# Chunked attention into a gated FFN: turned tiles written in a row, earlier clears, other load order, last store in two pieces

## The chip, the cores and the metric

The kernel runs on one core of one Trainium2 chip. The core has TensorE (PE, matrix products into PSUM), VectorE (DVE), ScalarE (ACT), GpSimd (POOL) and SyncE (SP, which here only issues transfers). The metric is the device time of one execution in microseconds, as the median of several runs.

## The reference

Queries attend by chunks of 32 tokens. A chunk sees 8 memory slots and the keys from 16 tokens before its start to 8 behind its end. The result, with the heads side by side, goes through an FFN with a ReLU gate.

```
q, k, v: (4, 8, 768, 64)      mem_k, mem_v: (4, 8, 8, 64)
for c in range(768 // 32):
    l, r = max(0, 32*c - 16), min(768, 32*c + 32 + 8)
    scores = q[:, :, 32*c:32*c+32] @ concat(mem_k, k[:, :, l:r]).T / 8
    a = softmax(scores)
    out[:, :, 32*c:32*c+32] = a @ concat(mem_v, v[:, :, l:r])
x = out as (3072, 512)
y = (relu(x @ w_gate) * (x @ w_val)) @ w_out        # d_ff = 1536
```

## The kernel before

The 3072 tokens are cut into eight blocks of 384 (half a sequence each), numbered 0 to 7. A block has 4 groups of 96 queries (`NQ`, `QB`), each against 128 key rows: 8 memory slots and a band of 120 tokens. Heads are taken in four pairs (`hp`). All matrix products are in f16 with f32 sums.

For every head pair the kernel needs keys and queries with the head dimension on partitions ("turned"). Blocks 0, 1 and 2 turn them on PE: `turn_pe` (L177) multiplies rows, held as 4 tokens per partition (`J` = 4), by a selection matrix `sel` (L191, keys) or by the identity `ident` (L196, queries). The product of step j is written to PSUM at every fourth column, so that the columns come out in token order. `turn_copy` (L199) has DVE cast them to f16: one copy of 896 elements for blocks 0 and 2 (L207), two for block 1 (L209, L210). Blocks 3 to 7 are turned by DMA (`turn_dma`).

The scores go to PSUM (`step_s0` for block 0, `step_s` for the others, both by `score_mms` L236), ACT takes the exponential. In blocks 0 and 1 `wide_d` (L279, L281) makes the sums and their logarithm, `wide_e` (L285) their inverse, `wide_v` (L292, L294) the weighted values, and DVE their product, `xT`. From block 2 on the value tile `vwins` carries ones in the upper half of its columns, so that values and sums come out of one product (`step_v`, L301). `one_words` (L447) writes these ones over the first two blocks' value tiles; for block 2 that is the code at L551 to L553, behind the last FFN unit of block 0.

The FFN of a block is 12 units of 128 hidden columns (L337; ACT's ReLU at L343, DVE's product at L344) and three output units of 128 tokens (`out_unit`, L362 to L367: 12 products, a copy by ACT, a store from ACT's queue).

The order is written out by hand: every engine runs its instructions in program order, and the framework adds the waits. Block 0's attention runs ahead of everything (L457 to L504, with products on a `filler` tile to occupy PE while loads are on their way). Then the FFN of block n is interleaved with the attention of block n+1 (L521 to L550 for the first, `run`, L580, for the rest). In `run` a turn of block 2 stands one unit ahead of its scores, and shares their PSUM tile `sc`.

Loads go through three queues. SP and ACT load the f32 rows of heads 0 to 3 for block 0 (`kst`, `qst`, L383, L384). POOL issues all others, casting to f16 on the way: first `memv`, then the rows of heads 4 to 7 (`load_rows`, L127, L128), then, behind the building of `ident` and `sel` (L433, L434), the values (`load_band`, L136), `memk` and the FFN's weights in six column slices (`load_w`, L166). A POOL load waits until the one eight before it has landed. SP copies the memory values into the value tiles (`load_mem_v`, L152).

Of the kernel before, what the change touches and what calls it, by code (L numbers as in the profile page):

```python
# [17 lines left out]
def kernel(  # L18
# [28 lines left out]
    J = 4  # L47
# [66 lines left out]
    def rows_of(n):  # L114
        if n not in rows:
            rows[n] = (half.tile([KR + 2, H, J * D], F16, tag="rk", name="rk"),
                       half.tile([QR, H, J * D], F16, tag="q16", name="rq"))
        return rows[n]

    def load_rows_mem(dma, dst, n, h0, nh):  # L120
        src = bass.AP(tensor=mem_k.tensor, offset=mem_k[n // 2, h0, 0, 0].offset,
                      ap=[[J * D, 2], [NMEM * D, nh], [1, J * D]])
        dma(dst, src)

    def load_rows(n, h0, nh):
        rk, rq = rows_of(n)
        pool_dma(rk[0:KR, h0:h0 + nh], k_rows(n, h0, nh))  # L127
        pool_dma(rq[:, h0:h0 + nh], q_rows(n, h0, nh))  # L128

    def load_band(n, src_t, dsts):  # L130
        b, p = divmod(n, 2)
        for i in range(NQ):
            m0, m1 = (16 if (p == 0 and i == 0) else 0), (112 if (p == 1 and i == NQ - 1) else BAND)
            src = bass.AP(tensor=src_t.tensor, offset=src_t[b, 0, TB * p + QB * i - 16 + m0, 0].offset,
                          ap=[[D, m1 - m0], [S * D, H], [1, D]])
            pool_dma(dsts[p][NMEM + m0:NMEM + m1, i, :, 0:D], src)  # L136

    def fetch_mem(dst, src_t):
        pool_dma(dst, bass.AP(tensor=src_t.tensor, offset=src_t[0, 0, 0, 0].offset,
                              ap=[[D, NMEM], [NMEM * D, B * H], [1, D]]))  # L140
# [33 lines left out]
    def bank(name):  # L174
        return pools["f"].tile([128, 512], F32, tag="f", name=name)

    def turn_pe(n, hp):  # L177

        if n != 1:
            pool, tag = (pools["t"], "t") if n == 0 else (sps, "sc")  # L180
            ps = pool.tile([128, 2, 512], F32, tag=tag, name="kq_ps")
            kps, qps = ps[:, 0], ps[:, 1, 0:TB]
        else:
            ps, kps, qps = None, bank("k_ps"), bank("q_ps")[:, 0:TB]
        turns[n, hp] = ps, kps, qps
        rk, rq = (t.rearrange("p h (j d) -> p h j d", j=J) for t in rows_of(n))
        sel = sels[n % 2].rearrange("p i t -> p (i t)")
        for j in range(J):
            kj = kps.rearrange("p (r j) -> p j r", j=J)[:, j]
            for hh in range(2):  # L190
                nc.tensor.matmul(kj[D * hh:D * hh + D], lhsT=rk[:, 2 * hp + hh, j], rhs=sel[0:KR + 2],  # L191
                                 start=True, stop=True)
        for j in range(J):
            qj = qps.rearrange("p (r j) -> p j r", j=J)[:, j]
            for hh in range(2):
                nc.tensor.matmul(qj[D * hh:D * hh + D], lhsT=rq[:, 2 * hp + hh, j], rhs=ident[:QR, :QR],  # L196
                                 start=True, stop=True)

    def turn_copy(n, hp):  # L199
        if n not in kTs:  # L200
            kq = turned.tile([128, HP, 512 + TB], F16, tag="kq", name="kq")
            kTs[n] = kq[:, :, 0:512].rearrange("p a (i m) -> p i a m", i=NQ)
            qTs[n] = kq[:, :, 512:].rearrange("p a (i m) -> p i a m", i=NQ)
            turns[n] = kq
        ps, kps, qps = turns.pop((n, hp))
        if n != 1:
            dve_copy(turns[n][:, hp], ps.rearrange("p a c -> p (a c)")[:, 0:512 + TB])  # L207
        else:
            dve_copy(turns[n][:, hp, 0:512], kps)  # L209
            dve_copy(turns[n][:, hp, 512:], qps)  # L210

    def turn_dma(n):
        kTs[n] = turned.tile([128, NQ, HP, 128], F16, tag="kT", name="kT")
# [25 lines left out]
    def step_s0(n, hp):  # L239

        sc = sps.tile([128, 2, 512], F32, tag="sc", name="sc_ps")
        mq = bass.AP(tensor=maskq.tensor, offset=maskq.offset, ap=[maskq.ap[0], [0, NQ], [1, QB]])
        for hh in range(2):
            nc.tensor.matmul(sc[:, hh, 0:TB].rearrange("p (i m) -> p i m", m=QB), lhsT=maskk, rhs=mq,
                             start=True, stop=False)
        score_mms(n, hp, sc, False)
        ex = epool.tile([128, 2, NQ, QB], F16, tag="ex", name="ex")
        nc.scalar.activation(ex.rearrange("p h i m -> p h (i m)"), sc[:, :, 0:TB], ACT.Exp, scale=SCALE)
        exs[n, hp] = ex
# [25 lines left out]
    def wide_d(n, hp):  # L275
        ex = exs[n, hp]
        for i0, i1, kind in ((0, 1, 1), (1, NQ, 0)) if n == 0 else ((0, NQ - 1, 0), (NQ - 1, NQ, 2)):
            for hh in range(2):
                nc.tensor.matmul(xs[D * hh:D * hh + D, QB * i0:QB * i1], lhsT=ones[:, kind, :],  # L279
                                 rhs=ex[:, hh, i0:i1, :], start=True, stop=True)  # L280
        nc.scalar.activation(xs, xs, ACT.Ln, scale=1.0 / 64.0)  # L281

    def wide_e(n, hp):
        rinv = rpool.tile([128, TB], F32, tag="rw", bufs=4, name="rw")
        nc.scalar.activation(rinv, xs, ACT.Exp, scale=-1.0, bias=mln64)  # L285
        rinvs[n, hp] = rinv
# [68 lines left out]

    def out_unit(n, t, between=()):
        o_ps = bank("o_ps")
        for m in range(NDC):
            if m == NDC // 2:
                for piece in between:  # L360
                    piece()
            nc.tensor.matmul(o_ps, lhsT=gvs[n][:, m, 128 * t:128 * t + 128], rhs=wo[:, m, :],  # L362
                             start=(m == 0), stop=(m == NDC - 1))
        o_sb = opool.tile([128, DM], F32, name="o_sb")
        nc.scalar.copy(o_sb, o_ps)  # L365
        row0 = TB * n + 128 * t
        act_dma(out[row0:row0 + 128, :], o_sb)  # L367

    def unit(n, u, between=()):
        if u < NDC:  # L370
# [7 lines left out]
            nc.tensor.matmul(xo, lhsT=filler[:, 0:128], rhs=filler[:, 0:TB], start=True, stop=True)  # L378


    nc.scalar.preload_act_table_set("natural_log_exp_and_others")
    for hp in range(HP // 2):
        sp(kst[0:KR, 2 * hp:2 * hp + 2], k_rows(0, 2 * hp, 2))  # L383
        act_dma(qst[:, 2 * hp:2 * hp + 2], q_rows(0, 2 * hp, 2))  # L384
        if hp == 0:
            load_rows_mem(sp, kst[KR:KR + 2], 0, 0, H // 2)
    fetch_mem(memv, mem_v)
    load_rows(0, 4, 4)
    load_rows_mem(pool_dma, rows_of(0)[0][KR:KR + 2, H // 2:H], 0, H // 2, H // 2)

    def words(t):
        return t.bitcast(U32)

    zero(words(ident), 0)
    zero(words(sels[0].rearrange("p i t -> p (i t)")), 0)
    zero(words(filler), 0)


# [21 lines left out]
    def select(ap, fill_with, base, pattern, mult, op=ALU.not_equal):  # L420
        nc.gpsimd.affine_select(out=ap, in_=ap, compare_op=op, fill=fill_with, base=base, pattern=pattern,
                                channel_multiplier=mult)

    def build_sel(p):

        s = sels[p]
        first_row = -6 if p == 0 else 10
        parts = [(0, NQ, 2, 32)] if p == 0 else [(0, NQ, 2, 30), (0, NQ - 1, 30, 32)]
        for i0, i1, t0, t1 in parts:
            select(s[:, i0:i1, t0:t1], 1.0, -first_row - t0, [[-24, i1 - i0], [-1, t1 - t0]], 1)  # L430
        select(s[:, :, 0:2], 1.0, -KR, [[0, NQ], [-1, 2]], 1)

    select(ident, 1.0, 0, [[-1, 128]], 1)  # L433
    build_sel(0)  # L434
    load_band(0, v, vwins)
    load_mem_v(0)
    fetch_mem(memk, mem_k)
# [19 lines left out]
    with tc.tile_pool(name="tps", bufs=2, space=bass.MemoryType.PSUM) as pools["t"]:  # L457
        fill(12)
        cast(0, 0, dve_copy)
        for t, hp in ((1, 0), (1, 1), (0, 1)):  # L460
            cast(t, hp, act_copy)
        turn_pe(0, 0)
        turn_copy(0, 0)
        fill(4)
        step_s0(0, 0)
        turn_pe(0, 1)
        turn_copy(0, 1)
        wide_d(0, 0)
        wide_e(0, 0)
        turn_pe(0, 2)  # L470
        step_s0(0, 1)
        turn_copy(0, 2)
        turn_pe(0, 3)
        turn_copy(0, 3)
    pools["f"] = ctx.enter_context(tc.tile_pool(name="fps", bufs=4, space=bass.MemoryType.PSUM))
    wide_d(0, 1)
    step_s0(0, 2)
    wide_e(0, 1)
    fill(1)
    step_s0(0, 3)  # L480
    wide_v(0, 0)
    wide_d(0, 2)
    wide_e(0, 2)


# [10 lines left out]

    ffn_open(0, (0, 1))
    wide_v(0, 1)
    chunk(0, 0)
    wide_d(0, 3)  # L500
    wide_e(0, 3)
    wide_v(0, 2)
    chunk(0, 1)
    wide_v(0, 3)  # L504
# [12 lines left out]
    def sums(n, hp):  # L517
        wide_d(n, hp)
        wide_e(n, hp)
# [23 lines left out]
    ffn_unit(0, 8)  # L543
    wide_v(1, 1)
    sums(1, 3)
    ffn_unit(0, 9)
    wide_v(1, 2)
    ffn_unit(0, 10)
    wide_v(1, 3)
    ffn_unit(0, 11)  # L550
    one_words(0, 0, 128, 0, NQ, ONE)  # L551
    one_words(0, 0, NMEM + 16, 0, 1, 0)
    one_words(0, 0, NMEM, 0, 1, ONE)  # L553
    load_band(2, v, vwins)
    load_mem_v(2)
    wo_src = moe_w_out.rearrange("(c p) f -> p c f", p=128)
# [87 lines left out]
```

## Time and profile before

| | |
|---|---|
| median of 5 runs | 241.1 us (240.81 to 242.24) |
| the profiled execution's own time | 242.24 us |
| its span | 239.3 us |
| PE busy | 230.1 us, 96% of the span |
| ACT busy | 142.8 us, 60% |
| DVE busy | 105.0 us, 44% |
| POOL busy | 100.2 us, 42% |
| granted PE clock, mean | 0.997 of full |
| DMA | 27.61 MB in 107655 packets |

The span is the stretch that the profiler saw; the execution's own time has some 3 us around it. Lines are those of the kernel before. In a group, "x64 | 4.3, 286" is the count, the busy time in us and the mean of one in ns. What follows the next bar is the idle time in front of the group and what ended it. In a timeline a line starts with its start and its duration in us.

### The profile page before, as it was taken

How to read it: one execution, taken by the hardware profiler on the slowest of the kernel's cores; microseconds unless marked ns; L12 is line 12 of the kernel's file. 1: busy time of each engine (PE TensorE's matmuls, PEld its weight loads, DVE VectorE, ACT ScalarE, POOL GpSimd, SP SyncE). 2: the span in 40 equal slices, each digit the busy share in tenths (PEclk: the TensorE clock that was granted, in tenths of full speed). 3: DMA queues.
4: the chain of work that ended last, by engine and by line, in shares of the span. 5: the costliest groups of instructions: out<-in, count | busy, mean ns of one | idle time of the engine just before them, and what ended most of it. 6: DMA issues, size and time to landing. Idle time of an engine off the chain costs nothing.

```text
span 239.3 us, 4598 instructions
## 1 busy us (share of the span) xinstructions
PE 230.1 (96%) x1737; PEld 133.6 (56%) x1737; DVE 105.0 (44%) x203; ACT 142.8 (60%) x300; POOL 100.2 (42%) x125
## 2 busy tenths in 40 slices
PE   7879999899999999999999999999999999999993
PEld 3635555455644566646664566556664666456641
DVE  4535646878621045512662146504652166313400
ACT  3564595277753388817984589728892698434321
POOL 7997667937039802990089302990040000000000
PEclk9999999999999999999999999999999999999998
DMA  7999999999979999799909997699902100120012
GB/s 160 152 177 195 186 186 189 178 192 146 141 119 116 200 152 143 47 166 124 184 13 126 151 178 68 45 191 148 139 3 78 53 3 0 44 90 0 1 44 88
DMA packets 107655, 27.61 MB, mean 115 GB/s; under 512 B 91682, under 2 KB 104562, under 8 KB 107634
## 3 DMA queue, kind: packets, MB, share of 16 engines
q0 software_dynamic: 82528, 15.16, 79.0%
q1 hardware_dynamic: 21234, 5.48, 20.5%
q10 hardware_dynamic: 3872, 6.69, 8.5%
q8 instruction: 13, 0.21, 0.3%
q14 instruction: 8, 0.07, 0.1%
HBM read 31.13 MB, written 6.29 MB: 156 GB/s over the span
## 4 chain that ended last, share of the span: by engine, by line
PE 83%; DVE 6%; POOL 3%; DMA 3%; ACT 2%; issue 1%; POOLq 0%; DVEq 0%
PE o_ps L362 26%; PE g_ps L337 24%; PE v_ps L337 24%; DMA wv<-in_moe_w_val_dram 3%; PE sc_ps L261 3%; PE xs_ps L301 2%; PE xo_ps L301 2%; DVE kq L207 2%; DVE gv L344 2%; POOL vwin L136 2%; DVE vwin L447 1%; PE sc_ps L236 1%; DVE kq L209 1%; ACT ln L305 1%; PE xo_ps L292 1%
## 5 line engine op out<-in xcount | busy, mean ns | idle before, releaser
L344 DVE TENSOR_TENSOR gv<-v_ps,gr 128x384 f16<-128x384 f32 x95 | 52.8, 557 | 99.6 <-ACT gr L343 85.9
L337 PE MATMUL v_ps<-xT,wv 128*128 128x384 f16 x380 | 78.3, 326 | 0.4 <-DMA wv<-in_moe_w_val_dram 0.2
L337 PE MATMUL g_ps<-xT,wg 128*128 128x384 f16 x380 | 78.4, 326 | 0.0
L362 PE MATMUL o_ps<-wo,gv 128*128 128x512 f16 x288 | 63.5, 379 | 0.0
L343 ACT ACTIVATE gr<-g_ps 128x384 f16<-128x384 f32 x95 | 46.2, 487 | 19.4 <-PE g_ps L337 10.3
L337 PEld LDWEIGHTS <-wv 128*128 128x128 f16 x384 | 36.1, 98 | 22.9 <-DMA wv<-in_moe_w_val_dram 1.4
L337 PEld LDWEIGHTS <-wg 128*128 128x128 f16 x384 | 36.0, 98 | 22.6
L362 PEld LDWEIGHTS <-gv 128*128 128x128 f16 x288 | 28.0, 98 | 33.0
L224 POOL COPY qbd<-qT 64x1536 f16<-64x1536 f16 x10 | 14.6, 1462 | 61.3 <-DMA qT<-q16n 61.0
L365 ACT COPY o_sb<-o_ps 128x512 f32<-128x512 f32 x24 | 14.1, 586 | 41.2 <-PE o_ps L362 37.2
L267 ACT ACTIVATE ex<-sc_ps,bias 128x256 f16<-128x256 f32 x84 | 33.4, 468 | 7.7 <-PE sc_ps L236 7.1
L136 POOL DMA_DIRECT2D vwin<-in_v_dram x32 | 29.0, 932 | 2.9 <-PE g_ps L337 1.0
L310 ACT ACTIVATE rinv<-ln,mln 64x768 f32<-64x768 f32 x24 | 22.2, 923 | 0.0
L305 ACT ACTIVATE ln<-xo_ps 64x384 f32<-64x384 f32 x24 | 11.7, 487 | 14.7 <-PE xs_ps L301 14.7
L136 POOL DMA_DIRECT2D k<-in_k_dram x20 | 17.8, 902 | 0.4 <-issue 0.4
L162 POOL DMA_DIRECT2D q16n<-in_q_dram x20 | 15.6, 800 | 5.0 <-DMA wo<-in_moe_w_out_dram 5.0
L316 DVE TENSOR_TENSOR xT<-xo_ps,rinv 64x384 f16<-64x384 f32 x24 | 13.1, 546 | 10.2 <-ACT rinv L310 10.2
L316 DVE TENSOR_TENSOR xT<-xs_ps,rinv 64x384 f16<-64x384 f32 x24 | 13.2, 551 | 0.7
L301 PEld LDWEIGHTS <-vwin 128*128 128x128 f16 x192 | 10.8, 98 | 3.2
L305 ACT ACTIVATE ln<-xs_ps 64x384 f32<-64x384 f32 x24 | 11.4, 474 | 0.0
L301 PE MATMUL xo_ps<-ex,vwin 128*128 128x96 f16 x96 | 11.1, 206 | 0.0
L301 PE MATMUL xs_ps<-ex,vwin 128*128 128x96 f16 x96 | 11.1, 206 | 0.0
(70 smaller groups left out, 136.3 us busy)
## 6 DMA issues: line engine op xcount, KB each, us to landing
out_dram<-o_sb ACTq DMA_DIRECT2D x24, 256.0 KB
vwin<-in_v_dram POOLq DMA_DIRECT2D x24, 120.0 KB, 8.9
q16n<-in_q_dram POOLq DMA_DIRECT2D x20, 96.0 KB, 5.2
k<-in_k_dram POOLq DMA_DIRECT2D x15, 120.0 KB, 5.0
wg<-in_moe_w_gate_dram POOLq DMA_DIRECT2D x6, 256.0 KB, 8.1
wv<-in_moe_w_val_dram POOLq DMA_DIRECT2D x6, 256.0 KB, 8.4
wo<-in_moe_w_out_dram POOLq DMA_DIRECT2D x3, 512.0 KB, 9.9
rk<-in_k_dram POOLq DMA_DIRECT2D x5, 224.0 KB, 7.7
```

What stands on the lines that cost most here:

```text
L136: pool_dma(dsts[p][NMEM + m0:NMEM + m1, i, :, 0:D], src)
L162: pool_dma(q16s[n][:, i], src)
L224: nc.gpsimd.tensor_copy(qbds[n % 2][s, :, :, hh, :].rearrange("p i a m -> p (i a) m"), qTs[n][s].rearrange("p i a m -> p (i a) m"))
L267: nc.scalar.activation(flat[:, :, :, s], view[:, :, :, s], ACT.Exp, scale=SCALE, bias=bias[:, g:g + 1])
L301: nc.tensor.matmul((xo, xs)[hh][:, QB * i:QB * i + QB], lhsT=vw[:, i, 2 * hp + hh, :], rhs=ex[:, hh, i, :], start=True, stop=True)
L305: nc.scalar.activation(ln[:, hh], (xo, xs)[hh][D:128], ACT.Ln, scale=1.0 / 64.0)
L310: nc.scalar.activation(rinv, lns.pop((n, hp)), ACT.Exp, scale=-1.0, bias=mln64[0:D, :])
L316: nc.vector.tensor_tensor(out=x_of(n)[D * hh:D * hh + D, hp, :], in0=(xo, xs)[hh][0:D], in1=rinv[:, hh, :], op=ALU.mult)
L337: nc.tensor.matmul(ps[a], lhsT=(wg, wv)[a][:, f, 128 * m:128 * m + 128], rhs=xTs[n][:, f, :], start=(f == 0), stop=(f == NFC - 1))
L343: nc.scalar.activation(gr, g_ps, ACT.Relu)
L344: nc.vector.tensor_tensor(out=gvs[n][:, m, :], in0=v_ps, in1=gr, op=ALU.mult)
L362: nc.tensor.matmul(o_ps, lhsT=gvs[n][:, m, 128 * t:128 * t + 128], rhs=wo[:, m, :], start=(m == 0), stop=(m == NDC - 1))
```

## The change

It has five parts.

1. In blocks 1 and 2 a turn's product j is written to PSUM in a row (columns 128 j or 96 j onward). The copy reads PSUM in permuted order, one element from each of the four rows in turn, and writes token order. Block 2 now takes two copies per turn, as block 1 did. Block 0 keeps the stepped write and its one copy.
2. The ones for block 2's value tile are written in pieces between the units 8 to 11 of block 0 in place of all behind unit 11.
3. ACT's table load stands behind its two query loads. POOL clears `ident` and `sel` itself, which DVE did, and builds them ahead of its loads. The rows of heads 4 to 7 are loaded by pairs of heads.
4. In block 0's attention the scores of pair 1 stand ahead of turn 2, the sums of pair 1 ahead of turn 3, the values of pair 0 ahead of the scores of pair 3, the sums of pair 3 ahead of the first FFN chunk; one filler product is gone.
5. The last store is made in two halves: DVE copies the left half, which SP stores, ACT copies and stores the right.

```diff
@@ turn_pe
-        for j in range(J):
-            kj = kps.rearrange("p (r j) -> p j r", j=J)[:, j]
-            for hh in range(2):
-                nc.tensor.matmul(kj[D * hh:D * hh + D], lhsT=rk[:, 2 * hp + hh, j], rhs=sel[0:KR + 2],
-                                 start=True, stop=True)
-        for j in range(J):
-            qj = qps.rearrange("p (r j) -> p j r", j=J)[:, j]
-            ...
+        for t, dst, w in ((rk, kps, sel[0:KR + 2]), (rq, qps, ident[:QR, :QR])):
+            steps = dst.rearrange("p (r j) -> p j r", j=J) if n == 0 else dst.rearrange("p (j r) -> p j r", j=J)
+            for j in range(J):
+                for hh in range(2):
+                    nc.tensor.matmul(steps[D * hh:D * hh + D, j], lhsT=t[:, 2 * hp + hh, j], rhs=w,
+                                     start=True, stop=True)
@@ turn_copy
-        if n != 1:
+        if n == 0:
             dve_copy(turns[n][:, hp], ps.rearrange("p a c -> p (a c)")[:, 0:512 + TB])
         else:
-            dve_copy(turns[n][:, hp, 0:512], kps)
-            dve_copy(turns[n][:, hp, 512:], qps)
+            for src, dst in ((kps, turns[n][:, hp, 0:512]), (qps, turns[n][:, hp, 512:])):
+                dve_copy(dst.rearrange("p (r j) -> p r j", j=J), src.rearrange("p (j r) -> p r j", j=J))
@@ out_unit
-        nc.scalar.copy(o_sb, o_ps)
-        act_dma(out[row0:row0 + 128, :], o_sb)
+        if last:
+            for s, copy, dma in ((slice(0, 256), dve_copy, sp), (slice(256, 512), act_copy, act_dma)):
+                copy(o_sb[:, s], o_ps[:, s])
+                dma(out[row0:row0 + 128, s], o_sb[:, s])
+        else:
+            nc.scalar.copy(o_sb, o_ps)
+            act_dma(out[row0:row0 + 128, :], o_sb)
@@ start
-    nc.scalar.preload_act_table_set("natural_log_exp_and_others")
     for hp in range(HP // 2):
         ...
-    fetch_mem(memv, mem_v)
-    load_rows(0, 4, 4)
-    load_rows_mem(pool_dma, rows_of(0)[0][KR:KR + 2, H // 2:H], 0, H // 2, H // 2)
+    nc.scalar.preload_act_table_set("natural_log_exp_and_others")
-    zero(words(ident), 0)
-    zero(words(sels[0].rearrange("p i t -> p (i t)")), 0)
     ...
+    nc.gpsimd.memset(words(ident), 0)
+    nc.gpsimd.memset(words(sels[0].rearrange("p i t -> p (i t)")), 0)
     select(ident, 1.0, 0, [[-1, 128]], 1)
     build_sel(0)
+    fetch_mem(memv, mem_v)
+    load_rows(0, 4, 2)
+    load_rows_mem(pool_dma, rows_of(0)[0][KR:KR + 2, H // 2:H], 0, H // 2, H // 2)
+    load_rows(0, 6, 2)
     load_band(0, v, vwins)
@@ block 0
+        step_s0(0, 1)
         turn_pe(0, 2)
-        step_s0(0, 1)
         turn_copy(0, 2)
+        wide_d(0, 1)
+        wide_e(0, 1)
         turn_pe(0, 3)
         turn_copy(0, 3)
     ...
-    wide_d(0, 1)
     step_s0(0, 2)
-    wide_e(0, 1)
-    fill(1)
-    step_s0(0, 3)
     wide_v(0, 0)
     wide_d(0, 2)
+    step_s0(0, 3)
     wide_e(0, 2)
     ...
     wide_v(0, 1)
-    chunk(0, 0)
     wide_d(0, 3)
     wide_e(0, 3)
+    chunk(0, 0)
@@ between the units of block 0
     sums(1, 3)
+    one_words(0, 0, 128, 0, 1, ONE)
     ffn_unit(0, 9)
     wide_v(1, 2)
+    one_words(0, 0, NMEM + 16, 0, 1, 0)
+    one_words(0, 0, NMEM, 0, 1, ONE)
     ffn_unit(0, 10)
     wide_v(1, 3)
+    one_words(0, 0, 128, 1, 2, ONE)
     ffn_unit(0, 11)
-    one_words(0, 0, 128, 0, NQ, ONE)
-    one_words(0, 0, NMEM + 16, 0, 1, 0)
-    one_words(0, 0, NMEM, 0, 1, ONE)
+    one_words(0, 0, 128, 2, NQ, ONE)
```

More of the change, by code (lines that the diff above doesn't have):

```diff
@@ L187, in turn_pe @@
         sel = sels[n % 2].rearrange("p i t -> p (i t)")
-        for j in range(J):
-            kj = kps.rearrange("p (r j) -> p j r", j=J)[:, j]
-            for hh in range(2):
-                nc.tensor.matmul(kj[D * hh:D * hh + D], lhsT=rk[:, 2 * hp + hh, j], rhs=sel[0:KR + 2],
-                                 start=True, stop=True)
-        for j in range(J):
-            qj = qps.rearrange("p (r j) -> p j r", j=J)[:, j]
-            for hh in range(2):
-                nc.tensor.matmul(qj[D * hh:D * hh + D], lhsT=rq[:, 2 * hp + hh, j], rhs=ident[:QR, :QR],
-                                 start=True, stop=True)
+        for t, dst, w in ((rk, kps, sel[0:KR + 2]), (rq, qps, ident[:QR, :QR])):
[4 more added lines that the diff above has]
+                                     start=True, stop=True)
     def turn_copy(n, hp):
@@ L357, in out_unit @@
         o_ps = bank("o_ps")
+        last = n == NB - 1 and t == NT - 1
         for m in range(NDC):
```

## The prediction

> **What bounds the kernel now.** I read the page first (engine shares, DMA row), then the chain that ended last from the start, then the groups with shapes kept apart, then the timeline around each place where TensorE (PE) stands still.
>
> ```profile
> span 239.3 us, 4598 instructions
> PE 230.1 (96%) x1737; PEld 133.6 (56%) x1737; DVE 105.0 (44%) x203; ACT 142.8 (60%) x300; POOL 100.2 (42%) x125
> ...
> DMA  7999999999979999799909997699902100120012
> ```
>
> PE is the engine that sets the end: from 82 us to 235.5 us its chain has no gap, so an edit counts only if it moves the moment at which that dense stretch begins, or the tail behind it. The DMA row (one digit is 6 us) says that the 16 DMA engines are 90% busy or more from 6 us to 66 us. In that stretch PE can't run ahead of its weights:
>
> ```profile
> 10.28 6.71 DMA wv<-in_moe_w_val_dram
> 16.99 0.05 issue
> 17.04 0.34 PE v_ps L337
> ```
>
> The first block's FFN starts when its first value weights land, at 16.99. The same happens twice more, and in the first of the two VectorE (DVE) is late at the same moment, since its copies of block 1 run back to back from 23.97 to 27.28:
>
> ```profile
> 26.73 0.55 DVE L210 CAST kq<-q_ps 128x384 f16<-128x384 f32 x1
> ...
> 27.32 0.44 PEld L337 LDWEIGHTS <-wv 128*128 128x128 f16 x4 [0.54 <-DMA wv<-in_moe_w_val_dram]
> 27.33 0.82 PE L337 MATMUL v_ps<-xT,wv 128*128 128x384 f16 x4 [0.16 <-DVE kq L210]
> ...
> 35.88 0.44 PEld L337 LDWEIGHTS <-wv 128*128 128x128 f16 x4 [0.40 <-DMA wv<-in_moe_w_val_dram]
> ```
>
> So up to 36 us the weights are the clock, and time that PE saves before is spent waiting. The next place is the largest stall that is left, 46.85 to 48.22, where DVE works off memsets ahead of the copy that block 2's first scores need:
>
> ```profile
> 42.79 1.67 DVE L447 MEMSET vwin<- 128x1024 uint32 x3 [0.16 <-issue]
> ...
> 44.46 0.27 DVE L559 MEMSET k<- 32x256 uint32 x1
> ...
> 44.82 0.27 DVE L560 MEMSET k<- 32x256 uint32 x1
> ...
> 45.85 0.91 DVE L447 MEMSET vwin<- 128x1024 uint32 x1 [0.16 <-issue]
> ...
> 47.09 1.08 DVE L207 CAST kq<-kq_ps 128x896 f16<-128x896 f32 x1
> ...
> 48.22 0.34 PE L236 MATMUL sc_ps<-kq 64*128 64x96 f16 x8 [1.37 <-DVE kq L207]
> ```
>
> **Part 1, the turns.** The groups give one matmul with 64 weight columns and 96 moving columns, written with a step of four elements (L196) and in a row (L292), and the copies:
>
> ```profile
> L196 PE MATMUL kq_ps<-ident,rq 96*64 96x96 f16 x64 | 4.3, 286 | 0.0
> ...
> L292 PE MATMUL xo_ps<-ex,vwin 128*64 128x96 f16 x64 | 2.9, 210 | 0.6 <-DVE xT L294 0.6
> ...
> L209 DVE CAST kq<-k_ps 128x512 f16<-128x512 f32 x4 | 2.7, 686 | 0.0
> ...
> L210 DVE CAST kq<-q_ps 128x384 f16<-128x384 f32 x4 | 2.2, 547 | 0.0
> ```
>
> In the timeline eight L196 take 0.33 us from first start to the next group (23.72 to 24.05), eight L292 take 0.19 us (34.59 to 34.78): the step costs 0.14. Eight L191 of 128 columns take 0.42 (23.30 to 23.72); in a row, by 128/96 of 0.19, 0.25: 0.17 less. So a turn falls from 0.75 to 0.44 us on PE, 2.5 us over eight turns. Almost none of it reaches the end. In block 1 the scores wait for DVE, whose chain starts with a product (L344, 23.48) that the turns don't move; the last turn's 0.31 is lost before 35.88, where the weights land. In block 2 each copy stands behind a product that waits for ScalarE's queue (L343 behind two L305), so it starts when it did.
>
> The permuted copy isn't in the trace: every DVE read of PSUM there is in a row. A copy takes 547 ns for 384 elements and 686 for 512, so 1.09 ns an element and about 0.13 fixed. The nearest row is PE's stepped write: eight L196 start 41 ns apart though each lasts 286, since the two halves of the partitions run side by side, so each has 82 ns for its 96 elements: 0.86 ns an element with a step, still faster than the copy goes. [...] A gain is excluded: no DVE row with a source in PSUM goes faster than this, in a row as they all are.
>
> For block 2 the one copy of 896 becomes two. From its start to the score the one takes 1.14 us (52.84 to 53.98), the pair in block 1 takes 1.21 (23.97 to 25.18): +0.07 for each of four turns.
>
> **Part 2, the ones' memsets.** One fill of 1024 elements, and the two small ones behind it, stood in one piece ahead of unit (1,0)'s product; half of the fill and both small ones now lie between the units 9 to 11, where DVE has gaps of 0.47 (38.24), 0.64 (39.73) and 0.68 us (41.39), and each memset is 0.27. What stays is a fill of 512: 0.49 by the two rows (0.27 for 256, 0.91 for 1024). The queue from 42.79 is 1.67 - 0.49 = 1.18 us shorter; PE is free by 46.4, so all of it counts: the copy starts at 45.91, the score at 47.12 in place of 48.22, 1.10 less. With +0.07 for the other three turns block 2 gives -0.89. If the gaps were filled, each memset would put off a product by 0.27, which the four PSUM banks let PE run past.
>
> **Part 3, the start.** GpSimd (POOL) now clears and builds the identity and selection before its loads. No POOL memset of that size is in the trace; its 128x1 ones take 0.10, a select over 128x128 0.29; I take 0.15 each. With the selects (0.29 + 0.65) the first load (memv) goes out at about 2.35 in place of 1.42. The rows of heads 4 to 7 were two loads (0.74, 0.68) and are four; with 0.57 for the smallest load as the floor, four of 0.60: +1.0. The selects no longer stand ahead of the v loads (-0.95). So the v loads (5.17) and all behind them, memk and the weights, are issued about 1.0 to 1.1 us later (wg at 10.6, not 9.49). Each POOL load waits for the one eight before it; two more in front shift the partners, but from memk on they are the same ones, and the new waits (third v load on memv, fourth on the first rows) are over by then.
>
> What that does to the landing: POOL's first packets flowed only at 4.6, when the k and q loads of SP and ACT let them, and wg's flowed at 12.0, behind the v packets. A load alone flows about 1.7 us after its issue begins (97.42 to about 99.2). At 10.6 wg's would be there at 12.2: 0.2 later, the rest being queue. Bounds: 0 if the queue still covers it, +1.1 if none of it does. I take +0.2.
>
> The order of block 0 (the score of head pair 1 ahead of turn 2, sums earlier) brings heads' sums forward, so behind the first value weights come 3.35 us to the end of chunk 3 where there are 3.56 now (17.04 to 20.6): with the landing at 17.2, 20.6 as before. The values of pair 0 are now asked for at 13.3 (now 15.09); v landed at about 13 and may make PE wait up to 0.5, hidden by the weights. The +0.2 comes back at 27.3 and 35.9, where later weights land; I count it once. The table load (1.28 us at 0.81) ran beside the query loads' issue (0.84 already); behind them it ends at 3.0, before ScalarE's first cast at 4.90: 0. Filler and first turn start 0.2 earlier, hidden by the weights too.
>
> **Part 4, the last store.** Today: copy 235.49, 0.59 us, issue at 236.10, packets from 236.9 to 237.75. In the changed program ScalarE's half copy waits for DVE's (a wait on DVE is in its list): DVE half at 256 x 1.09 + 0.13 = 0.41, to 235.9; ScalarE's half 0.39 (487 ns for 384 at L343, 586 for 512 at L365), to 236.34; second issue 236.36, 0.26 later than now, but half the packets (-0.42). -0.1, ends -0.4 and +0.3.
>
> **Sum.** +0.2 - 0.89 - 0.1 = -0.8 us, on a profiled execution of 242.24 us (span 239.3 and 2.9 around it): 241.4, span 238.5. That execution was the slowest of five; against the median of 241.1 it is 240.3. A change under 0.5% (1.2 us) counts as none here.
>
> **Rivals.**
> [...]
> 2. The loads aren't covered: POOL's later start leaves DMA engines idle near 4 to 12 us, weights land up to 1.1 later, and values of pair 0 wait besides: 1.1 in place of 0.2, so +0.1 in all: 241.2; with POOL memsets of 0.4 each (+0.5) and a wait for v that isn't hidden (+0.5), 242.2 and above. For it: 363 GB/s from 3 to 4 us, so the first loads finish early. Against: the queue in front of wg.
> 3. PE's turns do pay: without POOL's packets the k and q loads of block 0 are done sooner, weights land no later, DVE's products aren't in front of the copies. Half of the turns' 2.5 us and no +0.2: -0.8 - 0.2 - 1.2 = -2.2, 238.9. Against: DVE is busy without a gap in front of 27.28.
> 4. Nothing arrives: the memsets only move the wait to ScalarE. Within rival 2's time.
>
> **Chances.** The sum holds 0.48 (its own range 239.0 to 241.6, 0.20 of it below 239.9); rival 3 0.20, faster; rival 1 0.19, slower; rivals 2 and 4 0.13, of which 0.06 slower. Faster 0.20 + 0.20 = 0.40, same 0.28 + 0.07 = 0.35, slower 0.19 + 0.06 = 0.25. For 8 in 10 the range takes rival 3 whole, rival 2, and rival 1 up to f = 1.6: 238.4 to 244.0.
>
> **What would show it.** Right: turn matmuls near 206 ns at 96 columns; permuted copies at 686 and 547 ns; the score behind block 2's first turn about 1.1 us earlier against the unit before; the first wv landing between 17.0 and 17.4. Wrong: permuted copies over 900 and 700 ns; a wait of PE for v at about 13.5 longer than 1 us; wv landing past 18; the last packets later than 2.3 us behind the last matmul.

## The result and the profile after

| | before | changed |
|---|---|---|
| median, runs of both side by side | 241.47 us (80 runs, 240.14 to 244.55) | 240.65 us (43 runs, 239.45 to 242.42) |
| profiled execution, its own time | 242.24 us | 239.98 us |
| span of it | 239.3 us | 238.1 us |

The ratio changed to before is 0.9969, with a 95% interval of 0.9957 to 0.9982: 0.31% faster, 0.75 us (the medians are 0.82 apart), and by the bound of 0.5% no change. The forecast was 240.3 us.

The page after, with the engine shares and the DMA row:

```profile
span 238.1 us, 4610 instructions
PE 227.4 (96%) x1736; PEld 131.4 (55%) x1736; DVE 105.5 (44%) x208; ACT 142.3 (60%) x300; POOL 101.6 (43%) x129
...
DMA  7999999999979999499939999499902100120012
```

PE has 2.7 us less to do (230.1 before), and the span is only 1.2 us shorter: part of what PE no longer does, it now waits. The groups of the changed kernel with shapes kept apart show the turns written in a row and the permuted copies (the mean of one, in ns, stands behind the comma):

```profile
L207 DVE CAST kq<-k_ps 128x512 f16<-128x512 f32 x4 | 2.7, 680 | 0.0
...
L193 PE MATMUL q_ps<-ident,rq 96*64 96x96 f16 x32 | 1.4, 206 | 0.0
L207 DVE CAST kq<-q_ps 128x384 f16<-128x384 f32 x4 | 2.2, 546 | 0.0
```

A matmul of 96 columns takes 206 ns (286 stepped), the permuted copies take 680 and 546 ns (686 and 547 in a row). So the permuted read costs nothing.

The chain that ended last has the first value weights in the same place, 0.47 us later than before (16.99):

```profile
10.97 6.50 DMA wv<-in_moe_w_val_dram
17.46 0.05 issue
17.51 0.34 PE v_ps L334
```

PE's timeline around the weights and at the first score of block 2 and the next one:

```profile
13.75 0.23 PE L289 MATMUL xo_ps<-ex,vwin 128*64 128x96 f16 x2 [0.34 <-DMA vwin<-memv]
...
16.51 0.36 PE L276 MATMUL xs_ps<-ex,ones 128*64 128x96 f16 x4 [1.08 <-ACT rw L282]
...
27.25 0.82 PE L334 MATMUL v_ps<-xT,wv 128*128 128x384 f16 x4 [0.18 <-DMA wv<-in_moe_w_val_dram]
...
35.89 0.82 PE L334 MATMUL v_ps<-xT,wv 128*128 128x384 f16 x4 [0.25 <-DMA wv<-in_moe_w_val_dram]
...
46.99 0.34 PE L233 MATMUL sc_ps<-kq 64*128 64x96 f16 x8 [0.50 <-DVE kq L207]
...
52.81 0.34 PE L233 MATMUL sc_ps<-kq 64*128 64x96 f16 x8 [0.51 <-DVE kq L207]
```

The two later waits for value weights end where they ended before (27.33, 35.88). The first score of block 2 is 1.23 us earlier than before (48.22) and the fourth 1.04 (64.46, before 65.50); with 0.16 at the last store, below, that is the whole gain of the profiled executions. Two things are new: at 16.51 PE stands still for 1.08 us for ScalarE, and each of the four scores of block 2 waits 0.50 us for its copy. Before, only the first of the four waited (1.37 us, behind the memsets); the trace puts down no wait to the other three.

DVE's queue ahead of the first of these copies:

```profile
42.69 0.48 DVE L451 MEMSET vwin<- 128x512 uint32 x1
43.16 0.27 DVE L564 MEMSET k<- 32x256 uint32 x1
...
44.55 0.91 DVE L451 MEMSET vwin<- 128x1024 uint32 x1 [0.16 <-issue]
...
45.79 1.14 DVE L207 CAST kq<-kq_ps 128x512 f16<-128x512 f32 x2
```

The fill of 1.67 us has become one of 0.48, and the copy (two of them) starts at 45.79, 1.30 earlier than before (47.09).

The last store in the timeline:

```profile
234.45 0.42 DVE L366 COPY o_sb<-o_ps 128x256 f32<-128x256 f32 x1 [7.14 <-DMA out_dram<-o_sb]
234.90 0.38 SPq L367 DMA_DIRECT2D out_dram<-o_sb  x1
234.91 0.37 ACT L366 COPY o_sb<-o_ps 128x256 f32<-128x256 f32 x1 [2.46 <-DVE o_sb L366]
```

ScalarE's half waits for VectorE's half. From the start of the first copy to the end of the span it is 3.65 us (238.1 - 234.45), before it was 3.81 (239.3 - 235.49).

### The profile page after: what moved, and what is told of

Same layout as the page of the kernel before. It is cut to its first block, busy times and chain, and to the rows that moved or that the text cites. A ratio compares the mean times of both kernels' runs of the same rounds, so it can differ in the third digit from the quotient of the medians.

```text
span 238.1 us, 4610 instructions
## 1 busy us (share of the span) xinstructions
PE 227.4 (96%) x1736; PEld 131.4 (55%) x1736; DVE 105.5 (44%) x208; ACT 142.3 (60%) x300; POOL 101.6 (43%) x129
## 4 chain that ended last, share of the span: by engine, by line
PE 79%; DMA 7%; POOL 5%; DVE 4%; issue 2%; ACT 2%; POOLq 0%; DVEq 0%
PE o_ps L360 25%; PE g_ps L334 23%; PE v_ps L334 23%; DMA wv<-in_moe_w_val_dram 6%; PE sc_ps L258 3%; DVE kq L207 2%; POOL vwin L136 2%; PE xo_ps L298 2%; PE xs_ps L298 2%; DVE gv L341 2%; DMA out_dram<-o_sb 1%; ACT ln L302 1%; ACT gr L340 1%; PE xo_ps L289 1%; POOL rk L127 1%
## 5 line engine op out<-in xcount | busy, mean ns | idle before, releaser
L369 ACT COPY o_sb<-o_ps 128x512 f32<-128x512 f32 x23 | 13.5, 586 | 39.2 <-PE o_ps L360 33.2
L302 ACT ACTIVATE ln<-xo_ps 64x384 f32<-64x384 f32 x24 | 11.7, 487 | 14.7 <-PE xs_ps L298 14.7
```

Source lines behind the costliest of these rows:

```text
L302: nc.scalar.activation(ln[:, hh], (xo, xs)[hh][D:128], ACT.Ln, scale=1.0 / 64.0)
```

## The experiments

Theory: the clears (part 2 of the change) carry the gain, the store (5) adds a little, the turns in a row (1) give nothing because VectorE's copies come late, and the start (3 and 4) costs little. Rivals: the start costs more than it shows in the one profile; the turns pay. Twelve kernels were run, in three groups of four, each group on one chip with its own runs of before (medians 241.51, 241.12 and 241.17 us). Times are medians. The ratio on record is to the runs of before in the same group, with its 95% interval; it is not the quotient of the two medians, and where the two differ in what they say, both are given.

### E1: the clears alone

The kernel before with the ones written between units 8 to 11.

```diff
     sums(1, 3)
+    one_words(0, 0, 128, 0, 1, ONE)
...
     wide_v(1, 2)
+    one_words(0, 0, NMEM + 16, 0, 1, 0)
+    one_words(0, 0, NMEM, 0, 1, ONE)
...
     wide_v(1, 3)
+    one_words(0, 0, 128, 1, 2, ONE)
     ffn_unit(0, 11)
-    one_words(0, 0, 128, 0, NQ, ONE)
-    one_words(0, 0, NMEM + 16, 0, 1, 0)
-    one_words(0, 0, NMEM, 0, 1, ONE)
+    one_words(0, 0, 128, 2, NQ, ONE)
```

> The kernel before with part 2 alone, the ones written in pieces. Theory (the whole gain is VectorE's shorter queue ahead of block 2's first copy): block 2's first score 1.2 us earlier, the span about 1.2 us shorter, ratio about 0.995, so a little faster than the full change. Rival (the gain comes from the turns or the start): under 0.3 us, ratio above 0.9985.

Measured: 240.22 us, ratio 0.9957 (0.993 to 0.9984). The clears alone give about 1.0 us. The interval takes in the 0.9969 of the whole change, so whether the rest adds up to nothing or to a loss this run can't say. The first score of block 2, expected 1.2 us earlier, came later in its profile (48.61): that execution had a mean granted clock of 0.993 and was late ahead of block 2. The stretch that the clears act on is from the first turn of block 2 to its first score; first before, whose score is at 48.22, then E1:

```profile
44.49 0.63 PE L191 MATMUL kq_ps<-sel,rk 114*64 114x128 f16 x8
```

```profile
46.18 0.63 PE L191 MATMUL kq_ps<-sel,rk 114*64 114x128 f16 x8
...
48.61 0.34 PE L236 MATMUL sc_ps<-kq 64*128 64x96 f16 x8
```

It is 3.73 us before and 2.43 in E1: 1.30 less, about as expected.

### E2: the turns stepped again

The changed kernel with the turns and copies of before in blocks 1 and 2.

```diff
-            steps = dst.rearrange("p (r j) -> p j r", j=J) if n == 0 else dst.rearrange("p (j r) -> p j r", j=J)
+            steps = dst.rearrange("p (r j) -> p j r", j=J)
...
-        if n == 0:
+        if n != 1:
...
-                dve_copy(dst.rearrange("p (r j) -> p r j", j=J), src.rearrange("p (j r) -> p r j", j=J))
+                dve_copy(dst, src)
```

> The full change with part 1 undone: stepped writes, one copy in block 2. Theory (the turns' time on TensorE is lost behind VectorE's copies, and two copies cost 0.07 each turn): the stall ahead of each of block 2's scores falls from 0.5 us to 0.2, the turns take 0.75 in place of 0.44, and the end comes 0.2 to 0.3 us earlier than with the full change, ratio about 0.996. Rival (turns in a row pay): 0.5 to 2 us later than the full change, ratio at or above 0.999.

Measured: 241.34 us, ratio 0.9969 (0.9947 to 0.999). The two disagree: the ratio is that of the changed kernel itself, but the quotient of the medians is 0.9993, and the median is 0.7 us above the changed kernel's 240.65, as the rival had it. The time alone doesn't settle this. Part of the distance may be the clock: 16 of its 22 executions had a mean granted clock under 0.995, of the changed kernel 24 of 44; in the others the median span is 238.5 us (6 executions) beside 238.25 (20). For block 2 the trace settles it. Its first and its fourth score in E2, then the fourth in the changed kernel, whose first is at 46.99:

```profile
48.09 0.34 PE L233 MATMUL sc_ps<-kq 64*128 64x96 f16 x8
...
65.37 0.34 PE L233 MATMUL sc_ps<-kq 64*128 64x96 f16 x8
```

```profile
64.46 0.34 PE L233 MATMUL sc_ps<-kq 64*128 64x96 f16 x8 [0.51 <-DVE kq L207]
```

That is 17.28 us in E2, as before (48.22 to 65.50), and 17.47 in the changed kernel: with the copies as late as here, turns in a row with their two copies lose 0.06 us a turn. The stall ahead of a score, expected to fall from 0.5 to 0.2 us, is about 0.1 in E2 (the product ahead ends at 53.77, its second score starts at 53.85).

### E3: the start alone

The kernel before with the changed loads and the changed order of block 0 (parts 3 and 4 of the change: table load, POOL's order, scores and sums brought forward).

> The kernel before with parts 3 and 4 alone, the start. Theory (the first value weights land 0.4 us later, and the landings at 27 and 36 us take up what is left): span within 0.3 us of before, ratio 0.999 to 1.001. Rival A (the later loads carry through): 0.4 us longer. Rival B (the earlier sums of block 0 carry through): 0.3 us or more shorter.

Measured: 242.37 us, ratio 1.0036 (1.0013 to 1.0059). That is 0.9 us slower, where no more than 0.3 either way was expected. The chain that ended last, in this profile:

```profile
10.91 7.88 DMA wv<-in_moe_w_val_dram
...
18.84 0.50 PE v_ps L334
19.34 0.32 PE g_ps L334
19.66 0.32 PE v_ps L334
```

The first value weights land at 18.79. And from then on matmuls take longer: a step of the chain is 0.32 us, in the changed kernel's profile it is 0.16. The granted clock of PE was 0.50 there, for two stretches of some 3.4 us up to 24 us.

### E4: the last store alone

```diff
+        if last:
+            for s, copy, dma in ((slice(0, 256), dve_copy, sp), (slice(256, 512), act_copy, act_dma)):
+                copy(o_sb[:, s], o_ps[:, s])
+                dma(out[row0:row0 + 128, s], o_sb[:, s])
```

> The kernel before with part 5 alone, the last store in halves. Theory (ScalarE's half waits for VectorE's, so the second issue is 0.25 us later but moves half the bytes): from the last matmul to the end of the span 0.1 to 0.2 us shorter, ratio about 0.9993. Rival (the two stores run side by side): 0.4 us or more shorter.

Measured: 241.27 us, ratio 0.999 (0.9969 to 1.001). The median is 0.24 us below before, with zero inside the interval. In its profile it is 3.64 us from the start of the first copy (234.76) to the end of the span (238.4), 0.17 less than before, as expected.

### E5 and E6: which half of the start costs

E5 has the loads alone, E6 the order of block 0 alone, both on the kernel before.

E5:

```diff
-    fetch_mem(memv, mem_v)
-    load_rows(0, 4, 4)
-    load_rows_mem(pool_dma, rows_of(0)[0][KR:KR + 2, H // 2:H], 0, H // 2, H // 2)
+    nc.scalar.preload_act_table_set("natural_log_exp_and_others")
...
-    zero(words(ident), 0)
-    zero(words(sels[0].rearrange("p i t -> p (i t)")), 0)
...
+    nc.gpsimd.memset(words(ident), 0)
+    nc.gpsimd.memset(words(sels[0].rearrange("p i t -> p (i t)")), 0)
     select(ident, 1.0, 0, [[-1, 128]], 1)
     build_sel(0)
+    fetch_mem(memv, mem_v)
+    load_rows(0, 4, 2)
+    load_rows_mem(pool_dma, rows_of(0)[0][KR:KR + 2, H // 2:H], 0, H // 2, H // 2)
+    load_rows(0, 6, 2)
```

E6:

```diff
-        turn_pe(0, 2)
         step_s0(0, 1)
+        turn_pe(0, 2)
         turn_copy(0, 2)
+        wide_d(0, 1)
+        wide_e(0, 1)
         turn_pe(0, 3)
...
-    wide_d(0, 1)
     step_s0(0, 2)
-    wide_e(0, 1)
-    fill(1)
-    step_s0(0, 3)
     wide_v(0, 0)
     wide_d(0, 2)
+    step_s0(0, 3)
     wide_e(0, 2)
...
     wide_v(0, 1)
-    chunk(0, 0)
     wide_d(0, 3)
     wide_e(0, 3)
+    chunk(0, 0)
```

> The kernel before with the moved loads alone (table load behind the query loads, two clears on GpSimd, the pool's loads behind them, heads 4 to 7 by pairs), block 0's order as before. E3 (loads and order together) came out 0.9 us slower than before. Theory L (the later loads carry the loss): the first value weights land about 0.5 to 1.0 us later, TensorE idles there longer, and the time is 0.5 to 0.9 us above before (242.0 to 242.4 where before is 241.5). Theory O (the order carries it): no more than 0.3 us from before (241.2 to 241.8). A mark that tells them apart beside the time: the share of executions in which the mean granted clock is under 0.9965, 24 per cent in before and 64 per cent in E3: about 60 per cent under L, about 25 under O.

> The kernel before with block 0's new order alone (scores and turns of pairs 1 to 3 in another order, the filler product gone, chunk 0 behind the sums of pair 3), loads as before. Theory O: the sums of pair 3 stand ahead of chunk 0 on TensorE and wait about 1.1 us for ScalarE, so that the time is 0.5 to 0.9 us above before (242.0 to 242.4 where before is 241.5), with about 60 per cent of the executions under a mean clock of 0.9965. Theory L: within 0.3 us of before (241.2 to 241.8), some 25 per cent under 0.9965. Of the two runs E5 and E6 one must carry the loss, or each a half of it.

Measured: E5 242.3 us, ratio 1.0049 (1.0013 to 1.0085); E6 241.03 us, ratio 1.0001 (0.9973 to 1.0029). The loads carry the loss, 1.2 us by the ratio (0.3 to 2.0 by its interval). The order costs nothing by the median, though its sums do wait the 1.1 us that theory O named. The first value weights, expected 0.5 to 1.0 us later in E5, landed at 17.10 in its profile, only 0.11 later than in the one of before; one landing says little, as the account of part 3 shows below. The mark of the clock did not tell the two runs apart: 7 of 12 executions of E5 and 5 of 12 of E6 had a mean clock under 0.995, where of before only 21 of 124 in the three groups had one.

E6 shows where the clock goes. The windows of one microsecond give the busy time of each engine (and its instructions), then PE's granted clock, the DMA share and GB/s:

```profile
15.00:16.00 1.00, 1.00 (x19) 0.53 (x19) 0.00 (x0) 0.70 (x2) 1.00 (x3) 1.00 1.31 172
16.00:17.00 1.00, 0.02 (x2) 0.00 (x0) 0.56 (x1) 1.00 (x2) 0.86 (x4) 1.00 1.44 180
17.00:18.00 1.00, 0.90 (x7) 0.49 (x7) 0.00 (x0) 0.53 (x2) 0.86 (x2) 0.77 1.48 181
18.00:19.00 1.00, 1.00 (x11) 0.38 (x9) 0.00 (x0) 0.58 (x1) 0.79 (x2) 0.50 1.43 189
19.00:20.00 1.00, 1.00 (x9) 0.46 (x6) 0.56 (x1) 0.00 (x0) 0.47 (x1) 0.50 1.45 196
20.00:21.00 1.00, 1.00 (x11) 0.35 (x9) 0.00 (x0) 0.00 (x0) 1.00 (x3) 0.53 1.44 194
21.00:22.00 1.00, 1.00 (x8) 0.54 (x7) 0.56 (x1) 0.00 (x0) 1.00 (x3) 1.00 1.45 194
```

PE's timeline has the two waits of this stretch:

```profile
14.66 0.36 PE L279 MATMUL xs_ps<-ex,ones 128*64 128x96 f16 x4 [0.48 <-ACT ex L248]
...
17.10 0.36 PE L279 MATMUL xs_ps<-ex,ones 128*64 128x96 f16 x4 [1.08 <-ACT rw L285]
```

PE idles from 16 to 17.1 us (the wait of 1.08 us for ScalarE that the changed kernel has at 15.4 to 16.5), and from about 17.5 to 21 the clock is 0.50 with PE busy throughout. Here the weights were not late.

### E7: everything but the start

The changed kernel with the loads of E5 and the order of E6 undone (the two diffs above, backwards).

> The changed kernel without the two parts at the start (loads and block 0's order as before): turns in a row with permuted copies in blocks 1 and 2, split clears, last store in halves. If the parts add up as measured one by one (clears -1.3, store -0.2, turns 0 to -0.3): 239.7 to 240.0 where before is 241.5, thus 0.7 to 0.9 us faster than the changed kernel (240.65), with about 25 per cent of the executions under a mean clock of 0.9965 against 55 of the changed kernel. If the start's parts pay only together with the others, it is at 240.6 or slower.

Measured: 239.99 us, ratio 0.994 (0.9912 to 0.9969), within what was expected. Against 0.9969 of the changed kernel the start takes back 0.29%, 0.7 us; but the two intervals meet, and by the medians, each against its own before, it is 1.13 beside 0.82, thus 0.3 us. That the start costs something is shown by E3 and E5, whose intervals lie above 1; how much is known only roughly. One of its 12 executions had a clock under 0.995, of the changed kernel 24 of 44.

### E8: block 2's turns one unit earlier

The changed kernel; only the unit at which a turn of block 2 and its copy stand is another.

```diff
-                    if u == at[hp] - 1:
+                    if u == at[hp] - 2:
```

> The changed kernel with block 2's turns and their copies one unit earlier, so that VectorE's copy ends before the scores that read it. Theory S (the copies that start late are what hides the turns' gain; TensorE stalls 0.50 us before each of the four scores of block 2): the four stalls go, -1.5 to -2.1 us against the changed kernel, 238.6 to 239.2 where that is at 240.65. Theory B (the stall is only moved: the earlier turn waits for its PSUM bank or ScalarE's exp comes later): within 0.4 us of the changed kernel, with new idle time of TensorE at the turn (no less than 0.3 us each).

Measured: 238.71 us, ratio 0.9899 (0.986 to 0.9939), 0.7% below the changed kernel's 0.9969: 1.7 us, with the two intervals apart. In PE's timeline none of the four scores of block 2 waits now; the first turn and the first, second and fourth score:

```profile
43.80 0.41 PE L193 MATMUL kq_ps<-sel,rk 114*64 114x128 f16 x8
...
47.03 0.34 PE L233 MATMUL sc_ps<-kq 64*128 64x96 f16 x8
...
52.28 0.34 PE L233 MATMUL sc_ps<-kq 64*128 64x96 f16 x8
...
63.03 0.34 PE L233 MATMUL sc_ps<-kq 64*128 64x96 f16 x8
```

From the first score to the fourth it is 16.00 us here and 17.47 in the changed kernel, 0.49 less per turn: the stall of 0.51 is gone, and nothing of size has taken its place. Theory S holds.

### E9 and E10: do turns in a row pay when the copy is out of the way?

E9 is E7 with E8's edit. E10 is E9 with E2's edit: stepped turns, plain copies.

> E7 (the changed kernel without the parts at the start) with block 2's turns one unit earlier, as in E8. If what the start costs (0.7 us between E7 and the changed kernel) and what the earlier turns give (1.9 us, E8) add: 237.9 to 238.3 where before is at 241.2, faster than E8 (238.7). If the earlier turns already take in the loss of the start: 238.6 to 238.9.

> E9 with the turns of blocks 1 and 2 stepped and the copies plain, as before the change. In E2 the turns in a row were worth nothing that could be measured beside 0.3 us of noise. If that was because the gain on TensorE ran into VectorE's late copy, then here, where the copy of block 2 is early, stepping costs the difference of the matmuls: four turns of block 2 at 0.75 instead of 0.44 us, +1.2 us against E9 (block 1's stay behind the copies). If the turns are hidden by something else too: within 0.4 us of E9.

Measured: E9 237.52 us, ratio 0.9853 (0.9818 to 0.9889); E10 239.12 us, ratio 0.9919 (0.9891 to 0.9948). E9 came out below its range for adding effects (237.9 to 238.3), by less than its interval is wide. Between E9 and E10 lie 1.6 us, where 1.2 was expected. PE's timeline, first E9, then E10:

```profile
42.76 0.41 PE L193 MATMUL kq_ps<-sel,rk 114*64 114x128 f16 x8
43.01 0.34 PE L193 MATMUL kq_ps<-ident,rq 96*64 96x96 f16 x8
...
45.99 0.34 PE L233 MATMUL sc_ps<-kq 64*128 64x96 f16 x8
...
61.99 0.34 PE L233 MATMUL sc_ps<-kq 64*128 64x96 f16 x8
```

```profile
42.14 0.63 PE L193 MATMUL kq_ps<-sel,rk 114*64 114x128 f16 x8
42.56 0.54 PE L193 MATMUL kq_ps<-ident,rq 96*64 96x96 f16 x8
...
45.73 0.34 PE L233 MATMUL sc_ps<-kq 64*128 64x96 f16 x8
...
62.85 0.34 PE L233 MATMUL sc_ps<-kq 64*128 64x96 f16 x8
```

From the first turn of block 2 to its fourth score it is 19.23 us in E9 and 20.71 in E10, 0.37 per turn. So in block 2 the 0.31 us that a turn in a row was forecast to save on PE arrive in full, and a little more, as soon as the scores don't wait for the copy. That E2 showed no gain there was the late copy, not the turn. (The profiled spans differ by less, 235.7 and 236.5 us: E9's execution came 0.62 us later to block 2, behind a wait of 1.21 us for value weights at 27.24 that E10's does not have.)

### E11 and E12: does the idle bring the clock down?

E11 is the changed kernel with nine filler products, written to a bank of unit 1 that its own first product overwrites. E12 has all of the change but the loads, with the fill and with E8's edit.

```diff
+    def fill_v(count):
+        for i in range(count):
+            nc.tensor.matmul(units[0][1][0][1], lhsT=filler[:, 0:128], rhs=filler[:, 0:TB], start=True, stop=True)
...
     wide_v(0, 1)
+    fill_v(6)
     wide_d(0, 3)
     wide_e(0, 3)
+    fill_v(3)
     chunk(0, 0)
```

> The changed kernel with nine filler products (128x384, about 0.16 us each) in the idle of TensorE at 15.4 to 17.4 us: six ahead of the sums of pair 3, three behind them. They compute nothing that is used. If the idle there is what brings the granted clock to a half for some 3.4 us: the share of executions with a mean clock under 0.995 falls from 55 per cent to 25 or less, and the median falls by 0.2 to 0.5 us (240.1 to 240.4 where the changed kernel is at 240.65). If the clock falls for another reason: 55 per cent as before, and the time within 0.2 us or above.

> All of the change but the loads (table load, clears on GpSimd and the pool's loads as before), with block 2's turns one unit earlier and the nine filler products. E6 said that block 0's order alone was 0.25 us better where the clock stayed at 1.00 and lost it again in the half of the executions where it did not. If the fill keeps the clock up: 237.6 to 238.1, the fastest of all, with under 25 per cent of the executions below a mean clock of 0.995. If the fill does not help: at or above E9.

Measured: E11 240.27 us, ratio 0.9951 (0.993 to 0.9972), with 1 of 12 executions under a clock of 0.995 where the changed kernel had 24 of 44; E12 237.8 us, ratio 0.9854 (0.9825 to 0.9884), with none of 6. Windows of E11:

```profile
15.00:16.00 1.00, 1.00 (x14) 0.60 (x12) 0.56 (x1) 1.00 (x2) 1.00 (x3) 1.00 1.32 155
16.00:17.00 1.00, 1.00 (x9) 0.48 (x8) 0.00 (x0) 0.56 (x2) 1.00 (x2) 1.00 1.43 184
17.00:18.00 1.00, 1.00 (x8) 0.29 (x8) 0.00 (x0) 0.77 (x2) 0.76 (x5) 1.00 1.44 184
```

PE is busy throughout and the clock stays at 1.00. The share of executions with a lowered clock fell as the idle theory had it. No kernel with the changed start and without the fill ran in this third group; before had the lowered clock in 3 of 20 executions there, in 18 of 104 in the others, so the group is not likely to explain it. The time is 0.4 us lower by the two ratios and by the raw medians, but by the medians against each kernel's own before only 0.1, and the intervals overlap: a gain in time is not shown. E9 and E12 are equal within noise (E12 was expected to be the fastest of all and is not), and both are 1.5% faster than the kernel before and 1.2% faster than the changed one. What they share is the change without its loads, and block 2's turns one unit earlier.

## Why the prediction was right, and where it was not

**The sum.** Forecast -0.8 us, measured 0.9969, -0.75. The sum was right, and one of its terms was not; that it came within 0.1 us all the same is luck, as the paragraph on why it held shows.

**Part 2, the clears: right.** Forecast: first score of block 2 1.10 earlier, 0.07 less at each of the other three. In the profile it is 1.23, then 1.17, 1.10 and 1.04 earlier (52.81, 58.64 and 64.46 against 53.98, 59.74 and 65.50): the loss per turn is 0.06 to 0.07. E1 has the clears alone at 1.0 us by its ratio and at 1.30 in the stretch that they act on.

**Part 1, the turns: right, and shown for block 2.** Matmuls at 206 ns, permuted copies at 680 and 546 ns (686 and 547 in a row): the nearest row, PE's stepped write of 0.86 ns an element beside the copy's 1.09, pointed the right way, and VectorE's permuted read of f32 showed no slowdown. PE's stepped write did take longer than that in a row, 286 against 206 ns a matmul. In block 2 the gain was lost to the copies as forecast. In block 1 the first score now waits 0.70 us for its copy (0.15 before, both at 25.2 to 25.5); in block 2 the stalls of 0.5 us are, but for about 0.1, the turn's 0.37 and the second copy's 0.07, turned into a wait. E8, and E9 beside E10, show that it was that. The range up to 244.0 takes in rival 1 (chance 0.19), permuted copies with up to f = 1.6 times the time of those in a row: that was an estimate of mine and no run shows the term; the copies ran at f = 0.99 and 1.00.

**Part 3, the loads: mis-sized.** The step that failed is "I take +0.2", with "the rest being queue". POOL was sooner than forecast (memsets 0.15 each as taken, memv issued at 1.83, not 2.35; value weights issued at 10.97 with 10.28 before, 0.7 later and not 1.0 to 1.1), and still the landing in the profile was 0.47 later, just outside the 17.0 to 17.4 that I had named. The profiles of all fourteen kernels point to a queue that covers little or nothing of the later issue. With the loads as before (before, E1, E4, E6, E7, E9, E10, E12) the first value weights take 5.7 to 7.5 us from issue to landing, median 6.3; with the loads moved (changed, E2, E3, E5, E8, E11) 6.2 to 7.9, median 6.45. They land at 16.0 to 17.8, median 16.5, and at 17.1 to 18.8, median 17.4. The flight varies by more than the shift, from 6.18 in E5 to 7.88 in E3, so a single pair of traces can't size it.

In the profile of the changed kernel the delay did not come back at 27.3 and 35.9, so one trace would have said 0. The runs say 0.9 us for the whole start (E3, 0.3 to 1.4 by its interval) and 1.2 for the loads (E5), and less in company with the other parts (E7 beside the changed kernel: 0.7 by the ratios, 0.3 by the medians). A second thing was missing from the step: with PE waiting for the weights or for ScalarE, the clock goes to a half in some executions (0.50 in the windows of E6, behind a wait of 1.08 us). How much of the loss is the clock and how much the landing isn't settled: in the executions of E3 and E5 whose clock stayed over 0.995 the median spans were still 239.6 and 240.0 us, against 239.1 and 238.9 of before in the same groups. Both were profiled in executions with a lowered clock, so the way by which that rest reaches the end was not seen.

**Part 3, block 0's order: the cost of 0 was right by the median (E6: 1.0001), but a wait was overlooked.** I named the wait for v at 13.3 (0.34 us at 13.75, as forecast at most 0.5) and not that the sums of pair 3, now ahead of chunk 0, need ScalarE's inverse of pair 2, which stands behind an exponential of pair 3: 1.08 us. "Hidden by the weights" holds for its time and not for what it does to the clock (0.50 in E6's windows).

**Part 4, the last store: right within noise.** Forecast -0.1, profile -0.16, E4 -0.24 with zero in its interval.

**Why the sum held all the same.** E7 has turns, clears and store together at 0.994, -1.45 us (-2.1 to -0.75), where the steps gave -0.99; the start then gives back 0.7, where they gave +0.2. Taken at their middle the two misses are of opposite sign and cancel. But E7's interval takes in -0.99, so only the start's miss is shown (E3 and E5). Added one by one (E1 -1.04, E4 -0.24, E3 +0.87; the turns were not run alone) the parts make -0.4, and the whole made -0.75; the interval of each is about half a microsecond to each side, so neither an interplay nor its absence is shown by that. The agreement with the forecast to 0.05 us is closer than any of these terms is known.

**The rivals.** Rival 1 (slow permuted read) falls to the two rows of 680 and 546 ns. Rival 2 was the right worry: the weights did land later than +0.2, though not by POOL's memsets (0.15 each) or a longer wait for v (0.34), and the clock was not in it. Rival 3 (the turns pay) falls for block 2 by the trace of E2; for block 1 the evidence is only that its first score now waits 0.70 us for the copy, and E2's time leaves up to 0.7 us open. Rival 4 (nothing arrives) falls, by E1.

## What to carry to other kernels

A saving on the engine that sets the end is only worth what the next producer allows: here what a turn saved turned into a stall of 0.5 us, and one unit more of lead between turn and scores, a change of one digit, gave 1.7 us. Ahead of a dense stretch of matmuls, a wait of one microsecond that is hidden behind a load can still cost time if it takes PE's clock down (to 0.50 behind the wait of 1.08 us in E6; 0.75 us between executions of the changed kernel); compare the granted clock over many executions before a start is called hidden, as a single profile may have missed it. A part that is costed at "about nothing" is worth a run of its own: the start was the only part with a loss, and by the ratios it hid half of the gain.

## What the hardware did that I had not expected

In seven of the fourteen profiles (E1, E2, E3, E5, E6, E7, E8) the granted clock of PE fell to 0.50 for one or two stretches of about 3.4 us, beginning at 16.5 to 18.9 us, during or within about a microsecond behind PE's waits there. For executions without a profile the mean clock has to stand for it: one such stretch takes 0.007 off the mean (3.4 us at half, in a span of some 240), while the half clock at the very end, as in the profile of before (0.52 from 238 us to the end at 239.3), leaves 0.997. Executions with a mean under 0.995:

| kernel | executions | kernel | executions |
|---|---|---|---|
| before (three groups) | 21 of 124 | E6, order alone | 5 of 12 |
| changed | 24 of 44 | E7, all but the start | 1 of 12 |
| E1, clears alone | 8 of 22 | E8, changed, turns earlier | 5 of 6 |
| E2, changed, turns stepped | 16 of 22 | E9, E7 with turns earlier | 2 of 6 |
| E3, start alone | 14 of 22 | E10, E9 with turns stepped | 1 of 9 |
| E4, store alone | 4 of 22 | E11, changed with the fill | 1 of 12 |
| E5, loads alone | 7 of 12 | E12, order, turns earlier, fill | 0 of 6 |

The kernels with the changed start and no fill (changed, E2, E3, E8) have it in 59 of 94 executions, those with the start of before (before, E1, E4, E7, E9, E10) in 37 of 195, those with the fill in 1 of 18. The split is not a clean one, since kernels with the start of before have it too, where the weights came late: in the profiles of E1 and E7 PE waits 1.06 and 1.00 us for them. For the changed kernel the median span was 238.25 us in the executions above 0.995, 239.0 where the mean was 0.988 to 0.995 (one stretch, as in the windows of E6), and 240.3 below that. In one stretch of 3.4 us at half speed 1.7 us of work are lost by that count; in the changed kernel 0.75 of it reached the end. The profile's waits for later weights (27.25, 35.89) are where the rest may have gone; that wasn't tried. In E6 the longest gap of PE from 14 us on was 1.08 us. With the wait of 0.48 us before it (for an exponential, at 14.2 to 14.7) PE stood idle for 1.56 us in that stretch, and the clock fell at 17.5. The amount alone doesn't decide it: in the profile of the changed kernel PE idled 1.45 us from 14 us to 17.51 (1.08 and 0.37) and the clock stayed at 1.00, while in E7's it fell at about 16.6 behind no more than that. What decides which executions are hit, no run here shows.
